# Pooled attention and a GELU MLP on one core: V fetched three groups ahead between two output stores, with another order of group 0

## The chip, the cores and the metric

The kernel runs on one core of one Trainium2 chip. The metric is the device time of one execution in microseconds (us); lower is better. TensorE (PE in the profile) multiplies matrices, VectorE (DVE), ScalarE (ACT) and GpSimd (POOL) do elementwise work, and SyncE (SP) issues nearly all transfers.

## The reference, cut to what matters

```python
# q, k, v: [8 batches, 8 heads, 576 positions, 64]; float32
k_p = k.reshape(B, H, 72, 8, 64).mean(axis=3)        # mean of each 8 positions
v_p = v.reshape(B, H, 72, 8, 64).mean(axis=3)
scores = q @ k_p.T / sqrt(64)                        # [576, 72] for each head
attn = softmax(scores)
x = (attn @ v_p), heads side by side                 # [4608, 512]
h = x @ w_in                                         # 512 -> 2048
g = gelu_tanh(h)
out = g @ w_out                                      # 2048 -> 512, [4608, 512]
```

## The kernel before, in words

The 4608 rows are worked through in nine groups of 512 rows. Groups 0 to 7 are the first 512 positions of each batch; a group called R gathers the last 64 positions of all eight batches. The order is 0, 1, 2, 3, 4, 5, 6, R, 7, and `n_` counts the place in that order.

The attention of the next group is hidden in the MLP of the current one. The MLP of a group is one long row of matmuls with numbered slots: slots 0 to 63 are the first layer (`hidden`, `hidden_two`, `hidden_fast`), slots 64 to 175 the second (`mlp`, L537 to L614; 7 products of 16 matmuls each). `at(hooks, slot, f, ...)` hangs a step in front of the matmul of that slot. This only sets the order in which instructions are written. Each engine then runs its own list in that order and waits where it needs another engine's result, and so does SP with its transfers. Nothing is rearranged later.

The steps that matter here, for the group after next or the next one:

- `load_kv` (L764) fetches the pooled operands' sources: K main part (1 MB), two halves of 128 KB, and V main part (1 MB), into a tile `kv` that has two buffers. `load_q` fetches 1 MB of queries. All are issued by SP, except the queries of R, which GpSimd issues.
- `pool` sums over 8 positions on VectorE in up to three adds (L149, L151, L152) and writes `kvb`. `k_transpose_dma` (L211) turns K's sums with a transposing transfer into `kTd`; `k_spread` (L218) lets GpSimd copy them into `kbd`. `spread_v` (L172) multiplies V's sums by masks into `vbd`.
- `cast_q` (L128) casts queries to bfloat16 in quarters; `q_transpose_dma` (L232) turns them into `qT`, `scores` (L248) multiplies, `exps` and `norm` (L257, L279) make the softmax in `eb`, `e_transpose_dma` (L306) turns it into `eT`, and `values` (L344) yields `xT`, the MLP's input.
- At the end of a group `store_pair` (L416) sends out two stores of 512 KB: the first after product 3 (of slots 144 to 159), the second after product 4 (slots 160 to 175), when ScalarE has copied its last part. Both read tiles named `osb`, of which there are two buffers.
- The fast groups (`hidden_fast`, places 3 to 8 of the order) use the same two `osb` buffers at their start as scratch: L501 writes one of them after the first product, L508 the other after the third. L508 can start when the second store of the group before has landed. It reads `x4`, an accumulator that TensorE continues at slot 28 (`S(3)`, a `c L475` group in the profile).

In `hidden_fast` the order of slots is: product into x4 (0 to 3), into y4 (4 to 7), two hidden blocks (8 to 15), `S(2)` into x4 (16), `S(1)` into y4 (20), a hidden block (24), `S(3)` into x4 (28), and so on.

Group 0 has nothing to hide behind: its attention is written out by hand (L640 to L749), in four blocks of 128 rows. Its copies out of PSUM go to VectorE or ScalarE as the argument says; `norm_two` splits a block's normalization between both; `spread_v` in three parts and the cast of blocks 2 and 3 go to GpSimd and VectorE. A one-element copy into `gate` (L720) makes GpSimd wait for block 0's normalization before it goes on with the second part of `spread_v`. Block 3's scores are hung into slot 4 of group 0's MLP (`first_s`), and `hidden_half` has an order of its own for its first eight matmuls, so that four of them need only the first half of `xT`.

Of the kernel before, what the change touches and what calls it, by code (L numbers as in the profile page):

```python
# [15 lines left out]
GELU_SET = "gelu_apprx_tanh_and_others"  # L16
# [3 lines left out]
def kernel(  # L20
# [21 lines left out]
    nc = tc.nc  # L42
# [4 lines left out]
    KO = DM // 128  # L47
# [3 lines left out]
    W = H * Sp  # L51
# [45 lines left out]
    def kv_tile(b):  # L97
        st[b]["kv"] = kvp.tile([128, NB, 8, D], F32, name="kv", tag="kv")
# [29 lines left out]
    def cast_q(g, j0, j1, eng):  # L128
        if "qb" not in st[g]:
            st[g]["qb"] = work.tile([128, 4, H, D], BF16, name="q_b", bufs=1)  # L130
        copy(eng, st[g]["qb"][:, j0:j1], st[g]["q"][:, :, j0:j1].rearrange("p h j d -> p j h d"))
# [91 lines left out]
    def q_transpose_pe(g, j, eng, tag):  # L223
        tp = psum.tile([128, HP, 128], BF16, name="tp", tag=tag, bufs=BUFS[tag])
        for pr in range(HP):
            nc.tensor.transpose(out=tp[:, pr, :],
                                in_=st[g]["qb"][:, j, 2 * pr:2 * pr + 2, :].rearrange("p h d -> p (h d)"),
                                identity=identb)
        copy(eng, st[g]["qT"][:, j], tp)
# [69 lines left out]
    def e_transpose_pe(g, j, eng, tag):  # L299
        tp = psum.tile([128, 5, 128], BF16, name="tp", tag=tag, bufs=BUFS[tag])  # L300
        for c in range(5):
            nc.tensor.transpose(out=tp[:, c, :], in_=eb[:, j, 128 * c:128 * c + 128], identity=identb)
        copy(eng, st[g]["eT"][:, j], tp)
# [83 lines left out]
    def hidden_half(g, fo, half, hook, s):  # L387

        c0 = 256 * half
        hp = psum.tile([128, 2, 256], F32, name="mm", tag="mm", bufs=4)  # L390
        order = [(0, 0), (0, 1), (1, 0), (1, 1), (0, 2), (0, 3), (1, 2), (1, 3)]
        for i, (f, ko) in enumerate(order if s == 0 else sorted(order)):
            hook(s + i)
            nc.tensor.matmul(out=hp[:, f, :], lhsT=w_in_b[:, ko, (fo + f) * 128:(fo + f + 1) * 128],  # L394
                             rhs=st[g]["xT"][:, ko, c0:c0 + 256],
                             start=(i == 0 if s == 0 else ko == 0), stop=(ko == KO - 1), skip_group_check=True)
        nc.scalar.activation(out=gT[:, fo:fo + 2, c0:c0 + 256], in_=hp, func=ACT.Gelu_apprx_tanh)

    def output(g, r, fo, o):
# [317 lines left out]
    norm_two(0, 0, 5)  # L717
    spread_v(0, nc.gpsimd, (0,))
    pool_pe(0, 7, 9, 1, nc.scalar)
    nc.gpsimd.tensor_copy(out=gate, in_=eb[:, 0, 128 * 5 - W:128 * 5 - W + 1])  # L720
    spread_v(0, nc.gpsimd, (1,))
    cast_q(0, 2, 3, nc.gpsimd)
    spread_v(0, nc.gpsimd, (2,))
    load_w_in(2)
    load_w_in(3)
    norm_two(0, 1, 5)
    e_transpose_pe(0, 0, nc.vector, "mm")
    q_transpose_pe(0, 2, nc.scalar, "mm")
    e_transpose_pe(0, 1, nc.vector, "mm")
    scores(0, 2)  # L730
    exps(0, 2)
    cast_q(0, 3, 4, nc.vector)
    for x in range(2):
        values_half(0, 0, x, [nc.vector, nc.scalar][x], "mm")
    q_transpose_pe(0, 3, nc.vector, "mm")

    def first_s():
        scores(0, 3)
        exps(0, 3)
        nc.scalar.preload_act_table_set(GELU_SET)  # L740
        norm(0, 2, nc.vector)
        norm(0, 3, nc.vector)

    def first_t(j):
        e_transpose_pe(0, j, nc.vector, "sc")
# [18 lines left out]
    def load_kv(n, parts=(0, 1)):  # L764
        if n != B - 1:
            b = B - 1 if n == R else n
            if 0 in parts:
                kv_tile(b)
                load_main(b, "k", 0, 4, nc.sync)
                load_half(b, "k", nc.sync)  # L770
                load_half(b, "v", nc.sync)
            if 1 in parts:
                load_main(b, "v", 0, 4, nc.sync)

    def at(hooks, s, f, *a):
        hooks.setdefault(s, []).append(lambda: f(*a))
# [4 lines left out]
        at(hooks, va, values, n, (0, 1), False)  # L781

    hooks = {}
    at(hooks, 4, first_s)
    at(hooks, 16, first_t, 2)
    at(hooks, 28, first_t, 3)
    at(hooks, 32, first_v)
# [43 lines left out]
    for n_, g in enumerate(seq):  # L831
        if n_ == 0:
            continue
        hooks = {}
        fast = n_ >= 3
        if n_ == 1:
            for i in range(1, 4):
                at(hooks, i, w_sums, i, 0, NP, nc.vector)
            at(hooks, 36, g_sums, 0, 4)
            at(hooks, 57, g_sums, 4, 6, (0,))  # L840
        elif fast:
            at(hooks, 41, g_sums, 0, 2, (0,))
            at(hooks, 57, g_sums, 2, 6, (0,))
            at(hooks, 65, g_sums, 6, 8, (0,))
            at(hooks, 65, g_sums, 0, 4, (1,))
        else:
            at(hooks, 20, g_sums, 0, 2)
            at(hooks, 36, g_sums, 2, 4)
            at(hooks, 57, g_sums, 4, 6, (0,))
        if not fast:  # L850
            at(hooks, 65, g_sums, 6, 8, (0,))
        at(hooks, 64 + 32, g_sums, 4, 8, (1,))
        if n_ + 1 < len(seq):
            n = seq[n_ + 1]
            b = B - 1 if n == R else n
            kv = n != B - 1
            if n_ == 1:
                for j in range(4):
                    at(hooks, 22 + 4 * j, cast_q, n, j, j + 1, nc.scalar)
                at(hooks, 35, qT_tile, n)  # L860
                at(hooks, 35, q_transpose_dma, n)
            if kv and not fast:
                t0 = 22 if n_ == 1 else 12
                at(hooks, t0, pool, b, 0, 5)
                at(hooks, t0, dup_k, b, 0, 5)
                at(hooks, t0, kT_tile, b, None)
                at(hooks, t0, k_transpose_dma, b)
                t1 = t0 + (16 if n_ == 1 else 24)
                at(hooks, t1, pool, b, 5, 9)
                at(hooks, t1, k_spread, b, [nc.gpsimd, nc.gpsimd])  # L870
                at(hooks, t1, spread_v, b, nc.gpsimd)
            elif kv:
                at(hooks, 5, pool, b, 0, 5, (0,))
                at(hooks, 17, pool, b, 0, 5, (1,))
                at(hooks, 17, dup_k, b, 0, 5)
                at(hooks, 17, kT_tile, b, None)
                at(hooks, 17, k_transpose_dma, b)
                at(hooks, 17, spread_gated, b)
                at(hooks, 40, k_spread, b, [nc.gpsimd, nc.gpsimd])
            if fast:  # L880
                at(hooks, 2, qT_tile, n)
                at(hooks, 2, q_transpose_dma, n)
            sc_at = [68, 68, 90, 90]
            for j in range(4):
                at(hooks, sc_at[j], scores, n, j)
                at(hooks, sc_at[j] + 1, exps, n, j)
            at(hooks, 80, eT_tile, n)
            for j in range(4):
                at(hooks, 80 if j < 2 else 92, norm, n, j, nc.vector if j > 1 else nc.gpsimd)
                at(hooks, 80 if j < 2 else 92, e_transpose_dma, n, j)  # L890
            at(hooks, 64 + 66, nc.scalar.preload_act_table_set, GELU_SET)
            at(hooks, 64 + 100, xT_tile, n)
            if n_ == 1:
                at(hooks, 64 + 100, values, n, (0,))
                at(hooks, 64 + 107, values, n, (1,))
            else:
                at(hooks, 64 + 104, values, n)
        if n_ + 2 < len(seq):
            n2 = seq[n_ + 2]
            s2 = 44 if n_ == 1 else 57  # L900
            for half, ahead in enumerate((3, 2)):
                if n_ + ahead < len(seq) and seq[n_ + ahead] == R:
                    if half == 0:
                        at(hooks, 9, q_tile, R)
                    at(hooks, 9, gate_queries, g)
                    at(hooks, 9, load_q, R, 2 * half, 2 * half + 2, nc.gpsimd)
            if n2 != R:
                at(hooks, s2, q_tile, n2)
                at(hooks, s2, load_q, n2, 0, 4, nc.sync)
            at(hooks, 64 + 52, cast_gated, n2)  # L910
            if n_ < 2:
                at(hooks, 64 + 100, qT_tile, n2)
                at(hooks, 64 + 100, q_transpose_dma, n2)
                at(hooks, 64 + 100, load_kv, n2, (1,))
            elif n2 != B - 1:
                b2 = B - 1 if n2 == R else n2
                at(hooks, 64 + 84, pool, b2, 5, 9, (0,))
                at(hooks, 64 + 97, pool, b2, 5, 9, (1,))
            if n_ == 1:
                at(hooks, 45, load_kv, n2, (0,))  # L920
            else:
                at(hooks, 28, load_kv, n2)
        mlp(g, hooks, n_ + 1 == len(seq), fast)


# [28 lines left out]
```

## Time and profile before

| What | Value |
|---|---|
| Time, median of 3 runs | 280.57 us (279.7 to 280.78) |
| The profiled execution's own time | 280.57 us |
| Its span in the profile | 278.6 us |
| Granted TensorE clock | 0.998 of full speed |
| PE busy | 269.8 us (97% of the span) |
| DVE busy | 221.7 us (80%) |
| ACT busy | 176.1 us (63%) |
| POOL busy | 81.9 us (29%) |
| Moved by transfers | 54.37 MB, 195 GB/s over the span |

How to read it: the difference of about 2 us between span and time lies around the profiled part. PE is busy for all but 8.8 us of the span. So a change pays only where it removes one of PE's few idle stretches, and it costs where it makes a new one. A transfer has two times in the profile: when SP issues it, and when it lands.

### The profile page before, as it was taken

Reading aid. Unit: us, or ns where it says so; the run is one execution under the profiler, and the core shown is the slowest. Engines: PE = TensorE matmul, PEld = TensorE weight load, DVE = VectorE, ACT = ScalarE, POOL = GpSimd, SP = SyncE. Lnnn points to the kernel's source line nnn. Section 1 sums busy time; section 2 is a strip of 40 time slices with the busy share of each in tenths; the row PEclk is TensorE's granted clock in tenths of the full one; section 3 lists DMA queues with packets and bytes.
Section 4 is the critical chain, followed back from the end, with each engine's and each line's share of the span. In section 5 each row is a group of like instructions: output and inputs, shape, how many; then the busy total and the mean of one; then the engine's idle time right before and its main releaser. Section 6 shows DMA issues by size and latency. Waiting matters only on the chain.

```text
span 278.6 us, 6579 instructions
## 1 busy us (share of the span) xinstructions
PE 269.8 (97%) x2686; PEld 192.2 (69%) x2686; DVE 221.7 (80%) x367; ACT 176.1 (63%) x264; POOL 81.9 (29%) x123
## 2 busy tenths in 40 slices
PE   7989999998999999999999999999999999999995
PEld 3678844445854588668866876588668966886684
DVE  5896869989956798989999979887989558955832
ACT  1576575588547764696469636955696469656820
POOL 4640282006510542314263445533223300300000
PEclk9999999999999999999999999999999999999999
DMA  7999999998999895999399978964752460243013
GB/s 227 310 189 287 367 385 226 301 353 212 233 223 243 258 279 137 175 303 249 120 218 271 279 138 209 238 194 122 166 161 49 125 151 2 49 101 99 1 41 113
DMA packets 67856, 54.37 MB, mean 195 GB/s; under 512 B 41458, under 2 KB 53746, under 8 KB 67826
## 3 DMA queue, kind: packets, MB, share of 16 engines
q1 hardware_dynamic: 65186, 50.67, 71.3%
q0 software_dynamic: 2496, 3.15, 6.1%
q8 instruction: 21, 0.34, 0.5%
q10 hardware_dynamic: 144, 0.13, 0.1%
q14 instruction: 9, 0.07, 0.1%
HBM read 36.70 MB, written 9.44 MB: 166 GB/s over the span
## 4 chain that ended last, share of the span: by engine, by line
PE 78%; DMA 9%; DVE 7%; ACT 2%; POOL 1%; SPq 1%; issue 1%; DVEq 0%; ACTq 0%
PE mm L587 29%; PE mm L383 17%; PE c L475 11%; PE mm L400 5%; PE mm L394 5%; PE xo L344 3%; PE x L587 3%; DMA kTd<-kvb 2%; DMA q_sb<-in_q_dram 2%; PE sc L248 2%; DMA qT<-q_b 2%; DMA out_dram<-osb 1%; DMA eT<-eb 1%; PE mm L532 1%; DVE den L264 1%; DVE eb L279 1%
## 5 line engine op out<-in xcount | busy, mean ns | idle before, releaser
L383 PE MATMUL mm<-xT,w_in_b 128*128 128x512 bf16 x304 | 70.0, 379 | 0.0
L587 PEld LDWEIGHTS <-gT 128*128 128x128 bf16 x512 | 48.3, 98 | 9.0 <-issue 1.4
L385 ACT ACTIVATE gT<-mm 128x512 bf16<-128x512 f32 x76 | 43.6, 599 | 14.6 <-PE mm L383 14.4
L383 PEld LDWEIGHTS <-w_in_b 128*128 128x128 bf16 x304 | 29.7, 98 | 30.9 <-issue 0.3
L587 PEld LDWEIGHTS <-stage 128*128 128x128 bf16 x384 | 37.6, 98 | 4.4
L92 ACT CAST xT<-xo 128x512 bf16<-128x512 f32 (+1 forms) x24 | 13.2, 610 | 29.1 <-PE xo L344 24.8
L587 PE MATMUL mm<-tw,gT 128*128 128x256 bf16 x240 | 30.0, 273 | 0.0
L587 PE MATMUL mm<-w_out_b,gT 128*128 128x256 bf16 x240 | 29.9, 273 | 0.0
L264 DVE TENSOR_REDUCE den<-e 128x8 f32<-128x576 f32 x36 | 26.3, 731 | 3.3 <-ACT e L257 3.3
L279 POOL TENSOR_TENSOR eb<-e,r 128x576 bf16<-128x576 f32 x14 | 15.8, 1150 | 44.5 <-DVE r L273 23.7
L257 ACT ACTIVATE e<-sc 128x576 f32<-128x576 f32 x36 | 22.4, 650 | 8.7 <-POOL eb L279 4.3
L92 ACT COPY osb<-mm 128x512 f32<-128x512 f32 x30 | 17.8, 592 | 15.1 <-PE mm L587 14.4
L587 PE MATMUL mm<-tw,stage 128*128 128x256 bf16 x224 | 26.7, 273 | 0.0
L149 DVE TENSOR_TENSOR kv<-kv 128x1024 f32<-128x1024 f32 (+3 forms) x19 | 22.6, 1190 | 4.1 <-DMA kv<-in_k_dram 2.6
L172 POOL TENSOR_TENSOR vbd<-kvb,vmask 128x256 bf16<-128x256 bf16 (+2 forms) x38 | 22.0, 600 | 5.6 <-DVE kvb L152 4.7
L475 PEld LDWEIGHTS <-ws 128*128 128x128 bf16 x192 | 18.8, 98 | 6.4 <-issue 0.6
L94 POOL CAST q_b<-q_sb 128x1024 bf16<-128x1024 f32 (+1 forms) x15 | 16.1, 1094 | 19.7 <-DMA q_sb<-in_q_dram 19.6
L94 POOL COPY kbd<-kTd 64x288 bf16<-64x288 bf16 x12 | 7.0, 585 | 36.8 <-DMA kTd<-kvb 36.5
L475 PE MATMUL c<-tt,ws 128*128 128x256 bf16 x144 | 17.7, 272 | 0.1
L435 DVE TENSOR_TENSOR stage<-gT 128x512 bf16<-128x512 bf16 (+1 forms) x25 | 13.7, 548 | 4.8 <-ACT gT L385 2.7
L279 DVE TENSOR_TENSOR eb<-e,r 128x576 bf16<-128x576 f32 x18 | 16.6, 920 | 0.6
L394 PE MATMUL mm<-xT,w_in_b 128*128 128x256 bf16 x128 | 15.6, 273 | 0.1
(107 smaller groups left out, 421.3 us busy)
## 6 DMA issues: line engine op xcount, KB each, us to landing
kv<-in_k_dram SPq DMA_DIRECT2D x7, 1024.0 KB, 7.8
q_sb<-in_q_dram SPq DMA_DIRECT2D x7, 1024.0 KB, 9.8
kv<-in_v_dram SPq DMA_DIRECT2D x6, 1024.0 KB, 9.5
out_dram<-osb SPq DMA_DIRECT2D x12, 512.0 KB, 3.1
out_dram<-osb SPq DMA_DIRECT2D x11, 256.0 KB, 3.3
kv<-in_v_dram SPq DMA_DIRECT2D x4, 512.0 KB, 10.2
w_in_b<-in_moe_w_in_dram POOLq DMA_DIRECT2D x4, 512.0 KB, 6.7
w_out_s<-in_moe_w_out_dram SPq DMA_DIRECT2D x2, 1024.0 KB, 13.6
```

Of the source, the lines that this page charges most:

```text
L92: eng.copy(out=out, in_=in_)
L94: eng.tensor_copy(out=out, in_=in_)
L149: add(out=t[:, :, 0:4, :], in0=t[:, :, 0:4, :], in1=t[:, :, 4:8, :], op=ALU.add)
L172: eng.tensor_tensor(out=vbd[p0:128, b, n0:n1, :].rearrange("p (c r) (hh d) -> p c (r hh) d", c=max(m, 1), d=D), in0=kvb[p0:128, 4 + c0:4 + ...
L257: nc.scalar.activation(out=e.rearrange("p (x h) s -> p x (h s)", x=2), in_=sc[:, :, 0:4 * Sp], func=ACT.Exp, scale=1.0 / 64.0)
L264: nc.vector.reduce_sum(out=den, in_=e, axis=AX.X)
L279: eng.tensor_tensor(out=o.rearrange("p (pr hh s) -> p hh pr s", hh=2, s=Sp), in0=e.rearrange("p (hh pr) s -> p hh pr s", hh=2), in1=r.rear ...
L383: nc.tensor.matmul(out=hp, lhsT=w_in_b[:, ko, fo * 128:(fo + 1) * 128], rhs=st[g]["xT"][:, ko, :], start=(i == 0), stop=(i == KO - 1))
L385: nc.scalar.activation(out=gT[:, fo, :], in_=hp, func=ACT.Gelu_apprx_tanh)
L394: nc.tensor.matmul(out=hp[:, f, :], lhsT=w_in_b[:, ko, (fo + f) * 128:(fo + f + 1) * 128], rhs=st[g]["xT"][:, ko, c0:c0 + 256], start=(i = ...
L475: nc.tensor.matmul(out=acc[:, m, :], lhsT=lhs(i, m), rhs=rhs(i), start=bool(fresh and i == 0 and m % 2 == 0), stop=(i == 1), skip_group_ch ...
L587: nc.tensor.matmul(out=xs[p] if acc is xs else acc[:, p, :], lhsT=lt, rhs=rt, start=bool(fresh and m == 0 and (p == 0 or (last and acc is ...
```

## The change

Three things are changed together.

First, V. Before, V's main part of the group two places ahead was fetched together with K, the halves and the queries, right after `kTd`'s transfer. After, from place 2 on, V of the group three places ahead is fetched at slot 175, which is between the two output stores on SP's list. This happens at the ends of places 2, 3 and 4 (groups 2, 3 and 4). At place 2 itself V of group 4 moves ahead of K of group 4 on SP's list.

Second, at place 1 the last quarter of group 2's queries is cast by GpSimd at slot 22, in place of ScalarE at slot 34; the other three stay on ScalarE at slots 22, 26 and 30.

Third, group 0: the wait on `gate` goes, GpSimd casts blocks 2 and 3 in one instruction of 128x1024, block 3's queries are turned before block 1's softmax, block 0's softmax is copied by ScalarE and block 2's queries by VectorE (they were the other way round), block 3's scores stand ahead of the MLP and not inside it, and the first hidden block has the plain order of matmuls.

```diff
@@ hidden_half
-        order = [(0, 0), (0, 1), (1, 0), (1, 1), (0, 2), (0, 3), (1, 2), (1, 3)]
-        for i, (f, ko) in enumerate(order if s == 0 else sorted(order)):
-            hook(s + i)
...
+        for f in range(2):
+            for ko in range(KO):
+                hook(s + 4 * f + ko)
...
@@ group 0
     spread_v(0, nc.gpsimd, (0,))
     pool_pe(0, 7, 9, 1, nc.scalar)
-    nc.gpsimd.tensor_copy(out=gate, in_=eb[:, 0, 128 * 5 - W:128 * 5 - W + 1])
     spread_v(0, nc.gpsimd, (1,))
-    cast_q(0, 2, 3, nc.gpsimd)
+    cast_q(0, 2, 4, nc.gpsimd)
     spread_v(0, nc.gpsimd, (2,))
...
-    e_transpose_pe(0, 0, nc.vector, "mm")
-    q_transpose_pe(0, 2, nc.scalar, "mm")
+    e_transpose_pe(0, 0, nc.scalar, "mm")
+    q_transpose_pe(0, 2, nc.vector, "mm")
+    q_transpose_pe(0, 3, nc.scalar, "mm")
     e_transpose_pe(0, 1, nc.vector, "mm")
     scores(0, 2)
     exps(0, 2)
-    cast_q(0, 3, 4, nc.vector)
     for x in range(2):
         values_half(0, 0, x, [nc.vector, nc.scalar][x], "mm")
-    q_transpose_pe(0, 3, nc.vector, "mm")
-
-    def first_s():
-        scores(0, 3)
-        exps(0, 3)
-        nc.scalar.preload_act_table_set(GELU_SET)
-        norm(0, 2, nc.vector)
-        norm(0, 3, nc.vector)
+    scores(0, 3)
+    sums(0, 2)
+    exps(0, 3)
+    nc.scalar.preload_act_table_set(GELU_SET)
+    norm(0, 2, nc.vector)
+    norm(0, 3, nc.vector)
...
-    at(hooks, 4, first_s)
@@ load_kv
+            if "kv" not in st[b]:
+                kv_tile(b)
             if 0 in parts:
-                kv_tile(b)
@@ place 1
-                    at(hooks, 22 + 4 * j, cast_q, n, j, j + 1, nc.scalar)
+                    at(hooks, 22 + 4 * (j % 3), cast_q, n, j, j + 1, nc.gpsimd if j == 3 else nc.scalar)
@@ loads of K and V
-            if n_ == 1:
-                at(hooks, 45, load_kv, n2, (0,))
-            else:
-                at(hooks, 28, load_kv, n2)
+            at(hooks, 45 if n_ == 1 else 28, load_kv, n2, (0,))
+            if n_ == 2:
+                at(hooks, 14, load_kv, n2, (1,))
+            if n_ > 1 and n_ + 3 < len(seq):
+                at(hooks, 64 + 111, load_kv, seq[n_ + 3], (1,))
```

More of the change, by code (lines that the diff above doesn't have):

```diff
@@ L390, in hidden_half @@
         hp = psum.tile([128, 2, 256], F32, name="mm", tag="mm", bufs=4)
-        order = [(0, 0), (0, 1), (1, 0), (1, 1), (0, 2), (0, 3), (1, 2), (1, 3)]
-        for i, (f, ko) in enumerate(order if s == 0 else sorted(order)):
-            hook(s + i)
-            nc.tensor.matmul(out=hp[:, f, :], lhsT=w_in_b[:, ko, (fo + f) * 128:(fo + f + 1) * 128],
-                             rhs=st[g]["xT"][:, ko, c0:c0 + 256],
-                             start=(i == 0 if s == 0 else ko == 0), stop=(ko == KO - 1), skip_group_check=True)
+        for f in range(2):
+            for ko in range(KO):
+                hook(s + 4 * f + ko)
+                nc.tensor.matmul(out=hp[:, f, :], lhsT=w_in_b[:, ko, (fo + f) * 128:(fo + f + 1) * 128],
+                                 rhs=st[g]["xT"][:, ko, c0:c0 + 256], start=(ko == 0), stop=(ko == KO - 1))
         nc.scalar.activation(out=gT[:, fo:fo + 2, c0:c0 + 256], in_=hp, func=ACT.Gelu_apprx_tanh)
```

## The prediction

> **What bounds the kernel now.** I read the busy line and the chain on the page first, then TensorE's timeline for its idle stretches, then who waits for transfers, then SP's list of issues.
>
> ```profile
> PE 269.8 (97%) x2686; PEld 192.2 (69%) x2686; DVE 221.7 (80%) x367; ACT 176.1 (63%) x264; POOL 81.9 (29%) x123
> PE 78%; DMA 9%; DVE 7%; ACT 2%; POOL 1%; SPq 1%; issue 1%; DVEq 0%; ACTq 0%
> ```
>
> PE is idle for 278.6 - 269.8 = 8.8 us in all. About 3.3 us of that lie after its last matmul (275.29). The timeline shows the idle stretches with their releasers in brackets; these five, and 1.07 and 0.69 us in the first 6 us, are the main ones:
>
> ```profile
> 14.48 0.40 PE L226 MATMUL tp<-identb,q_b 128*128 128x128 bf16 x4 [0.55 <-POOL q_b L94]
> 15.56 0.42 PE L241 MATMUL sc<-kbd,qT 128*128 128x144 bf16 x4 [0.23 <-ACT qT L92]
> 66.77 0.45 PE L248 MATMUL sc<-kbd,qT 64*64 64x72 bf16 x32 [0.83 <-DMA qT<-q_b]
> 163.90 0.97 PE L344 MATMUL xo<-eT,vbd 32*64 32x256 bf16 x24 [0.64 <-DMA eT<-eb]
> 180.15 0.45 PE L248 MATMUL sc<-kbd,qT 64*64 64x72 bf16 x30 [0.59 <-POOL kbd L94]
> ```
>
> After 17 us only 0.83 + 0.64 + 0.59 = 2.06 us of idle time can be won. So everything turns on new idle time. The chain shows where PE has no slack though it isn't idle:
>
> ```profile
> 110.68 4.04 DMA out_dram<-osb
> 114.82 1.02 ACT osb L508
> 115.84 0.04 issue
> 115.88 1.03 PE c L475 x8
> ```
>
> That is the start of place 3: the second store of place 2 lands at 114.72, L508 may then write `osb`, and S(3) starts as L508 ends. A store that lands later there moves PE by as much. The waits agree (us in total, times, longest):
>
> ```profile
> ACT osb L508 <- DMA out_dram<-osb: 2.4, 3, 1.0
> ```
>
> **Part 1, group 0.** Removed: the gate copy (0.19) with its wait (0.58), two casts of 128x512 (GpSimd 0.61, VectorE 0.42). Added: one GpSimd cast of 128x1024; rows of that shape have a mean of 1.15, the slowest near here 1.51. The second half of q landed at 13.27, so the cast runs from 13.3 to 14.4-14.8; block 2's quarter alone was ready at 14.42. Block 3's query turn (0.41 on PE) now stands ahead of block 1's softmax turn. On ScalarE the softmax copy (0.59 for 512 columns, so about 0.7 for 640, an estimate) and one query copy (0.59) queue behind the three normalizations that ended at 14.89: about 16.2, against 15.51 for the one copy before. Block 3's scores (0.25) move ahead of the first hidden matmul: equal work, so 17.28 + 0.25 = 17.53 is the mark to compare with. I get the first hidden matmul at 17.6 to 18.2, a loss of 0.1 to 0.7, taken 0.4. Without the gate VectorE's first normalization runs beside GpSimd: 0.83 as the second did, not 0.53; ScalarE's share ended at 13.42 anyway.
>
> This loss is covered by the 0.83 idle at 66.77. What releases PE there is a chain without PE: group 2's queries landed at 57.62, the casts start at 57.70. Their load was issued at 48.90, behind softmax turns that SP could not issue faster, because loads from the start (V of group 1) landed only at 46.10. If that cover were gone, the 0.4 would count in full.
>
> **Part 2, the cast at place 1.** The fourth ScalarE cast ran from 60.71 to 61.33 and `qT` was issued at 61.36. After, ScalarE's third ends near 60.33, and GpSimd, idle for the 17.4 us before 65.01, casts from 57.7 for 0.6 to 0.9 us (rows of 128x512: 0.61, 0.86). SP issues `kTd` from 59.62 to 60.84, so `qT` is issued at 60.9 at the earliest: 0.46 won at most. Against it: the trace's transfer records show `qT`'s packets from 64.0 to 66.1, following at once on `kTd`'s last (63.9), so the issue may not have been the limit. And VectorE's adds for `kTd` run beside the cast: an add of 128x1024 took 1.87 and 1.75 beside casts twice this long, 1.25 without, so half of 0.55 is 0.3 lost. I take 0.1 won (from 0.46 won to 0.2 lost).
>
> [...]
>
> **Part 3, V between the stores.** Bytes are unchanged. Each of three loads (ends of places 2, 3, 4) now stands ahead of the second store on SP's list. What a load in front of a store does is seen once in this trace, at the end of place 1:
>
> ```profile
> 82.43 0.57 SPq L112 DMA_DIRECT2D kv<-in_v_dram  x1
> 83.09 0.49 SPq L416 DMA_DIRECT2D out_dram<-osb  x1
> 84.41 1.77 SPq L211 DMA_TRANSPOSE kTd<-kvb  x1
> ```
>
> That store's landing, then the one at 138.35, from the answers for the store's line in those windows:
>
> ```profile
> DMA to landing us min/median/max: 9.4/9.4/9.4
> DMA to landing us min/median/max: 3.0/3.0/3.0
> ```
>
> In the packet records V's 512 packets of 2 KB run from 83.6 to 88.4 and the store's 4 KB packets begin as they end: the queue works in order. At a steady rate (95 packets in 0.5 us, from 120 on) V needs 2.7 us; this one, with a slow start, needed 4.8. At place 1 that hurt nobody, since place 2 isn't fast and writes `osb` late. The three new ones precede fast places.
>
> Place 3: the first store's packets end at 110.25. V then holds the queue until 112.95 to 115.05; the second store's began at 111.45. Delay 1.5 to 3.6, slack none: 2.4 taken, between the ends, as the loads after transposes start slowly but not all as slowly as that one.
>
> Place 4: first store's packets end at 137.95, V until 140.7 to 142.8, second store's began at 139.15: delay 1.55 to 3.65. Slack: landing 141.35 to L508 at 141.84 is 0.5, and L508's end to S(3) another 0.5. Cost 0.5 to 2.6, taken 1.4.
>
> Place 5: 165.05, then 167.75 to 169.85, against 167.55: delay 0.2 to 2.3; slack 0.9 likewise. At the same time the 0.64 idle at 163.90 goes: `eT` was issued at 159.88 and took 4.0 to land, against 2.6 in undisturbed places, because q landed only at 160.04; with V's 2.7 us out of that burst it lands before PE asks. But PE then comes 0.64 sooner to the same store, and the slack shrinks by it. Cost 0 to 2.0, less 0.64: taken +0.2 in sum (-0.64 to +1.4). Late next: `kTd`, whose landing at 178.26 made the 0.59 at 180.15. It queues behind `qT`, which queues behind that store: 0 to 1.0, taken 0.3.
>
> [...]
>
> Place 2's V of group 4 ahead of K: both were already issued back to back behind `kTd` (86.23 to 89.67) and neither is needed before place 3's first slots; K landed at 95.93, so V's 2.7 us are hidden. Taken at nothing; if K's pool at 111.09 waited it would cost PE only through `kTd`, 60 slots later.
>
> Sum: -0.1 + 2.4 + 1.4 + 0.2 + 0.3 = +4.2. The profiled execution took 280.57, which is also the median of the runs: 284.8 us. The ends: -0.46 + 1.5 + 0.5 - 0.64 = +0.9, and 0.2 + 3.6 + 2.6 + 1.4 + 1.0 = +8.8, so 281.5 to 289.4 in this case.
>
> **Rivals.** (a) The store isn't held: V drains before the second store's packets would start, or the engines overlap them. Then the 0.64 goes, and 0.1 to 0.46 at place 1: 279.5 to 279.8. With the 0.59 at 180.15 gone too, 278.9. For it: at place 5 the stores are 4 us apart, and the first store's packets leave the queue empty at 138.0 to 139.0. Against it: 9.4 us. It decides if V holds the queue under about 1.2 us, and no row shows that.
>
> (b) The store is held, but L508's delay is caught up: PE finds other idle time to give back. Against it: after place 5 PE has almost none. It would leave at most 1 us: 281 to 282.
>
> (c) Group 0's loss isn't covered and is the only effect beside (a): 280.0 to 280.6.
>
> **How the numbers follow.** The store held, as summed: 0.70. (b) 0.08, (a) 0.15, (c) 0.07. About 0.5% (1.4 us) is what a measurement of this kernel can tell from no change, so faster means below 279.17: half of (a), 0.08. Same is the rest of (a), (c), and some of (b) and of the low end of the main case: 0.20. Slower: 0.72. Range: 279.6 to 288.0 leaves out most of (a)'s faster half and the case of all upper ends together.
>
> **What would show it.** Right: the second stores of places 2, 3 and 4 land 5 to 7 us after issue; ACT osb L508 waits for out_dram by 2 to 4 us at places 3 and 4; PE idle before c L475 there, released by L508; the idle at 163.90 gone; PE's other work unchanged. Wrong: second stores landing in 3 to 4 us, L508 waiting under 1 us, or idle time before the first hidden matmul that carries through 66 us.

## The result, and the profile after

The changed kernel takes 289.02 us (median of 6, 287.41 to 290.63) against 280.13 us (279.02 to 281.25) for the kernel before: a ratio of 1.031, 95% interval 1.026 to 1.036. It is slower, as forecast, but by 8.9 us and not by 4.2; that is above the top of the range (288.0). The profiled execution took 288.41 us with a span of 286.7 us, 8.1 us more span than before.

From the page of the changed kernel, the busy line and the chain's shares:

```profile
PE 271.6 (95%) x2686; PEld 192.9 (67%) x2686; DVE 222.1 (77%) x365; ACT 175.3 (61%) x264; POOL 80.1 (28%) x123
PE 75%; DMA 16%; DVE 4%; ACT 3%; issue 1%; SPq 1%; POOL 0%; ACTq 0%; DVEq 0%
```

PE's idle time grew from 8.8 to 15.1 us (286.7 less 271.6), and transfers now hold 16% of the chain instead of 9%. PE is also busy 1.8 us longer with the same 2686 matmuls. These are two effects. The idle stretches come first, from TensorE's timeline (start, us, what ran; in brackets the idle time before it and its releaser):

```profile
67.02 0.45 PE L248 MATMUL sc<-kbd,qT 64*64 64x72 bf16 x32 [0.60 <-DMA qT<-q_b]
119.24 1.03 PE L474 MATMUL c<-tt,ws 128*128 128x256 bf16 x8 [3.17 <-ACT osb L507]
149.30 1.03 PE L474 MATMUL c<-tt,ws 128*128 128x256 bf16 x8 [2.44 <-ACT osb L507]
179.09 1.87 PE L474 MATMUL c<-tt,ws 128*128 128x256 bf16 x8 [2.09 <-ACT osb L507]
180.75 1.88 PE L383 MATMUL mm<-xT,w_in_b 128*128 128x512 bf16 x4
```

PE now stands before S(3) at places 3, 4 and 5: 3.17 + 2.44 + 2.09 = 7.70 us. The old stretches of 0.64 (before `xo`, 163.90) and 0.59 (180.15) are gone. L507 is the copy that was L508 before. The chain shows what it waits for, the second store of the group before:

```profile
110.92 7.16 DMA out_dram<-osb
...
141.71 6.43 DMA out_dram<-osb
...
171.85 6.08 DMA out_dram<-osb
...
179.09 1.87 PE c L474 x8
```

The stores land 7.16, 6.43 and 6.08 us after their issue; at the first of these places it was 4.04 before. The waits (us in total, times, longest) agree: 2.4 us with a longest of 1.0 became

```profile
ACT osb L507 <- DMA out_dram<-osb: 11.4, 4, 4.1
PE c L474 <- ACT osb L507: 7.7, 3, 3.2
```

The second effect stands in the last two lines of the timeline: after the third idle stretch the same matmuls take 1.87 and 1.88 us instead of 1.03. The windows by engine have the granted clock in them (us, then busy time of PE, PEld, DVE, ACT and POOL, PEclk, DMA share, GB/s):

```profile
175.65:179.06 3.41, 1.35 (x9) 0.69 (x7) 2.42 (x4) 1.03 (x2) 3.27 (x7) 1.00 1.23 311
179.06:182.47 3.41, 3.38 (x13) 1.79 (x13) 1.23 (x1) 1.42 (x2) 1.91 (x4) 0.50 1.02 143
182.47:185.88 3.41, 3.41 (x25) 2.35 (x24) 2.20 (x4) 3.01 (x4) 0.84 (x2) 1.00 1.11 317
```

For 3.41 us the clock is halved: PE's 3.38 us of work there would have taken half as long, so 1.7 us are lost. In the profiled execution of the kernel before the clock record, which starts 4.4 us into the span, shows the whole clock until PE's last matmul is done.

The span's 8.1 us put together: +0.25 by the first scores of group 2 (67.02 against 66.77), +3.11 to S(3) of place 3, +2.60 at place 4, +1.35 at place 5 (1.99 of delay less the 0.64 gone), then +1.7 from the halved clock and -0.59 from the idle time gone at 180.15, and -0.3 in all the rest.

### The profile page after: what moved, and what is told of

Read it like the earlier page. It is cut to its first block, busy times and chain, and to the rows that moved or that the text cites. A ratio compares the mean times of both kernels' runs of the same rounds, so it can differ in the third digit from the quotient of the medians.

```text
span 286.7 us, 6575 instructions
## 1 busy us (share of the span) xinstructions
PE 271.6 (95%) x2686; PEld 192.9 (67%) x2686; DVE 222.1 (77%) x365; ACT 175.3 (61%) x264; POOL 80.1 (28%) x123
## 4 chain that ended last, share of the span: by engine, by line
PE 75%; DMA 16%; DVE 4%; ACT 3%; issue 1%; SPq 1%; POOL 0%; ACTq 0%; DVEq 0%
PE mm L586 30%; PE mm L383 19%; PE c L474 10%; DMA out_dram<-osb 7%; PE mm L399 5%; DMA w_out_s<-in_moe_w_out_dram 5%; PE x L586 2%; PE xo L344 2%; PE sc L248 2%; DMA q_sb<-in_q_dram 2%; DMA qT<-q_b 2%; PE mm L531 1%; ACT xT L92 1%; PE mm L394 1%; ACT osb L507 1%
## 5 line engine op out<-in xcount | busy, mean ns | idle before, releaser
L383 PE MATMUL mm<-xT,w_in_b 128*128 128x512 bf16 x304 | 71.0, 382 | 0.0
L279 POOL TENSOR_TENSOR eb<-e,r 128x576 bf16<-128x576 f32 x14 | 15.8, 1149 | 50.3 <-DVE r L273 28.3
L149 DVE TENSOR_TENSOR kv<-kv 128x1024 f32<-128x1024 f32 (+3 forms) x19 | 23.4, 1231 | 4.1 <-DMA kv<-in_k_dram 2.6
L92 ACT COPY osb<-mm 128x512 f32<-128x512 f32 x30 | 17.8, 593 | 14.2 <-PE mm L586 13.5
L474 PE MATMUL c<-tt,ws 128*128 128x256 bf16 x144 | 18.5, 280 | 7.7 <-ACT osb L507 7.7
L435 DVE TENSOR_TENSOR gT<-gT 128x512 bf16<-128x512 bf16 (+1 forms) x25 | 13.0, 519 | 3.5 <-ACT gT L385 1.4
```

Of the source, the lines that this page charges most:

```text
L92: eng.copy(out=out, in_=in_)
L149: add(out=t[:, :, 0:4, :], in0=t[:, :, 0:4, :], in1=t[:, :, 4:8, :], op=ALU.add)
L279: eng.tensor_tensor(out=o.rearrange("p (pr hh s) -> p hh pr s", hh=2, s=Sp), in0=e.rearrange("p (hh pr) s -> p hh pr s", hh=2), in1=r.rear ...
L383: nc.tensor.matmul(out=hp, lhsT=w_in_b[:, ko, fo * 128:(fo + 1) * 128], rhs=st[g]["xT"][:, ko, :], start=(i == 0), stop=(i == KO - 1))
L474: nc.tensor.matmul(out=acc[:, m, :], lhsT=lhs(i, m), rhs=rhs(i), start=bool(fresh and i == 0 and m % 2 == 0), stop=(i == 1), skip_group_ch ...
```

## Experiments

The theories have letters in the texts on record. **Q**: V's bytes stand in SP's queue ahead of the second store, and whatever next writes that store's buffer stops PE. **K**: a long idle stretch halves PE's clock for a while, which costs beside the idle time. **X**: R's queries, issued by GpSimd, and the transposing transfers, issued by SP, slow each other when they move together. **Y** and **Z** are two reasons why V holds the queue so long: because SP is issuing the transposing transfer right behind it (Y), or by itself (Z).

### One part alone

`e1_v_alone` is the kernel before with the change's edits to `load_kv` and to its calls, nothing else:

```diff
+            if n_ > 1 and n_ + 3 < len(seq):
+                at(hooks, 64 + 111, load_kv, seq[n_ + 3], (1,))
...
```

> The kernel before with the V loads of the change alone (place 2 at slot 14, and between the two stores at the ends of places 2, 3 and 4). Theory Q (the second store waits on SP's queue behind V's 1 MB, and L508 waits for the store): all of the loss is here; second stores of places 2 to 4 land 6 to 7.5 us after issue, PE idle before S(3) by 3.2, 2.4 and 2.1 us (each within 0.7), time 287 to 290. Theory G (group 0 or the cast carries a good part of the loss into the later groups): under 285.

Measured: 288.37 us, ratio 1.028 (1.021 to 1.035). In the profiled execution PE waits 3.54, 2.36 and 1.58 us for L508 before S(3) at places 3 to 5. `e2_without_v` is the changed kernel with V loaded as before, so group 0 and the cast alone:

```diff
-            at(hooks, 45 if n_ == 1 else 28, load_kv, n2, (0,))
...
+            if n_ == 1:
+                at(hooks, 45, load_kv, n2, (0,))
+            else:
+                at(hooks, 28, load_kv, n2)
```

> The changed kernel with the V loads put back as before, so group 0 and the cast alone. Theory Q: 280.1 plus 0.2 to 0.5, so 280.2 to 281, no idle time before S(3). Theory G: 283 or more.

Measured: 279.67 us, ratio 0.998 (0.992 to 1.004). So nearly the whole loss is V's place on the queue; group 0 and the cast together can't be told from nothing.

### Other places for the two transfers

`e3_v_after_store` issues V right behind the second store instead of ahead of it:

```diff
-                at(hooks, 64 + 111, load_kv, seq[n_ + 3], (1,))
+                last_load.append(seq[n_ + 3])
         mlp(g, hooks, n_ + 1 == len(seq), fast)
+        for n in last_load:
+            load_kv(n, (1,))
+        last_load.clear()
```

> The changed kernel with the three V loads issued right after the second store, not before it. Theory Q: second stores land in 3 to 4 us again, PE's idle before S(3) under 0.3 us at each place; qT and kTd queue behind V, so up to 1.5 us idle before the scores at places 3 to 5; time 279.5 to 282.5. Theory T (the first microseconds of a fast group can't bear another 1 MB in whatever order): the loss comes back before the scores, 285 or more.

Measured: 293.55 us, ratio 1.049 (1.043 to 1.055): worse, against what I expected. The store was free again (it landed 3.1 us after its issue) and the idle time before S(3) was gone, but PE now waited before the scores:

```profile
156.11 0.27 PE L248 MATMUL sc<-kbd,qT 64*64 64x72 bf16 x2 [5.14 <-POOL kbd L94]
191.19 0.27 PE L248 MATMUL sc<-kbd,qT 64*64 64x72 bf16 x2 [4.87 <-POOL kbd L94]
```

V's bytes had moved ahead of `qT` and `kTd`, and at places 4 and 5, where GpSimd issues R's queries, those ran at the same time as `qT`. In the packet records R's 128 packets of 4 KB took 751 and 799 ns each on the mean at these two places, against 251 and 234 in the kernel before, where `qT` was already through, and 159 for those of a store alone. Of `qT`'s 256-byte packets 2 to 126 started in each 0.5 us there, instead of 400 to 570. `qT` landed 15.8 us after its issue (174.62 to 190.43). At place 3, which has no such queries, there was no wait.

`e4_store_on_act` takes the store away from V by another queue: ScalarE issues it.

```diff
-                store_pair(g, 1, osb[1])
+                store_pair(g, 1, osb[1], eng=nc.scalar if g in (2, 3, 4) else nc.sync)
```

> The changed kernel with the second store of groups 2, 3 and 4 issued by ScalarE instead of SP; V stays where it is. Theory Q (order on one queue): the store no longer stands behind V, shares the engines with it and lands 3.5 to 5.5 us after issue; idle before S(3) 0 to 1.5 us at each place, time 280.5 to 284. Theory B (the bytes themselves, not their order, fill the engines): the store still lands after 6 us or more, time 287 or more.

Measured: 300.14 us, ratio 1.072 (1.065 to 1.079), the worst of all and not the 280.5 to 284 that I expected. ScalarE's timeline at place 3:

```profile
111.05 0.37 ACTq L415 DMA_DIRECT2D out_dram<-osb  x1
111.76 1.02 ACT L500 COPY osb<-c 128x1024 f32<-128x1024 f32 x1 [0.74 <-DMA out_dram<-osb]
...
122.62 1.01 ACT L507 COPY osb<-c 128x1024 f32<-128x1024 f32 x1 [8.40 <-DMA out_dram<-osb]
```

The store landed 11.5 us after its issue. Its first packet began only at 115.00, 3.95 us after the issue, among V's last ones. Then its packets ran beside `qT`'s on SP's queue until 122.06: 20 of the 128 took 0.5 to 3.3 us each, the others 0.16 to 0.28. `qT` landed 14.2 us after its own issue. So here a second queue was no way past the first: the store took 11.5 us in place of the 7.16 of the changed kernel, and `qT` 14.2 in place of 9.2.

### Is it the buffer, and does it go by bytes?

`e5_scratch_swapped` lets the fast places meet the held buffer later, at slot 36 instead of S(3) at 28:

```diff
-        k2, k0, k1 = part(), part(), spare
+        k2, k0, k1 = part(), spare, part()
```

> The changed kernel with the scratch of a fast group swapped: L507 (the former L508) writes the spare buffer, and the tile of the second store is first written by the VectorE copy L510, which TensorE needs only at slot 36. V stays between the stores. Theory Q (the late store costs time only through that one wait): V and the stores land as in the changed kernel (second store 6 to 7.2 us after issue), but PE's idle time before slot 28 goes, and before slot 36 1.7 us less is left per place, so 1.5, 0.7 and 0.4 us; time 281 to 284. Theory D (transfers in general are late, and the next wait takes over in full): 287 or more.

Measured: 284.10 us, ratio 1.016 (1.010 to 1.022). The stores land nearly as late as in the changed kernel (6.65 us after issue at place 3, 6.0 at places 4 and 5), but PE waits at slot 36, and less:

```profile
118.44 1.03 PE L474 MATMUL c<-xT,ws 128*128 128x256 bf16 x8 [1.14 <-DVE osb L510]
146.99 1.03 PE L474 MATMUL c<-xT,ws 128*128 128x256 bf16 x8 [0.45 <-DVE osb L510]
175.73 1.03 PE L474 MATMUL c<-xT,ws 128*128 128x256 bf16 x8 [0.53 <-DVE osb L510]
```

The wait went where the buffer went. `e6_half_of_v` leaves half of V between the stores and fetches the other half behind K:

```diff
-                at(hooks, 64 + 111, load_kv, seq[n_ + 3], (1,))
+                at(hooks, 64 + 111, load_kv, seq[n_ + 3], (1,), (0, 2))
+            if 2 < n_ < 6:
+                at(hooks, 28, load_kv, n2, (1,), (2, 4))
```

> The changed kernel with half of V (512 KB) between the stores and the other half at slot 28 of the next place, behind K. Theory Q by bytes: the store lands some 2.5 us sooner than in the changed kernel, idle before S(3) 0.7, 0.2 and 0 us, time 280 to 282.5. Theory P (any load there costs a fixed part, not by bytes): idle before S(3) 2 us or more at each place, time 286 or more.

Measured: 280.68 us, ratio 1.004 (1.001 to 1.006). The store at place 3 lands 4.63 us after its issue, and PE waits for it at one place only:

```profile
PE c L474 <- ACT osb L507: 0.6, 1, 0.6
```

With half the bytes the 7.70 us are 0.63. Both runs carry Q.

### The clock

`e8_filler` keeps PE busy with eight matmuls that nobody uses, ahead of S(3) at the three places:

```diff
+        if g in (3, 4, 5):
+            warm_up(8, "mm")
         product(x4, 0, S(3), T(t3), 28)
```

> The changed kernel with 8 matmuls of 128x512 on zeros (1.7 us) ahead of S(3) at places 3, 4 and 5: extra work for TensorE, in the time in which it waits. Theory K (idle time of 2 to 3 us costs a second time, because TensorE's granted clock is then halved for a stretch of 3.4 us, 1.7 us each): granted clock 0.998 or more, idle time that is left before S(3) under 1.5 us, time 285.5 to 287.5, below the changed kernel's 289. Theory N (the halved clock has nothing to do with idle time): clock still 0.98 to 0.994, time 288 to 291.

Measured: 287.22 us, ratio 1.028 (1.023 to 1.032). The store is held as before (ScalarE still waits 11.0 us for it in all), but the granted clock is 0.998 to 1.000 in all four executions, where all six of the changed kernel had 0.982 to 0.994. The loss of the medians is 7.4 us instead of 8.9. The difference of 1.5 us is near the 1.7 worked out from the trace, but the two intervals overlap, so that the times alone don't show it; the clocks do.

### R's queries

`e7_v_after_r_on_sp` is `e3_v_after_store` with R's queries issued by SP behind the gate's transfer, so that nothing moves on GpSimd's queue there; `e10_r_on_sp` is the same edit in the kernel before.

```diff
-                    at(hooks, 9, load_q, R, 2 * half, 2 * half + 2, nc.gpsimd)
+                    at(hooks, 28, load_q, R, 2 * half, 2 * half + 2, nc.sync)
```

> The run with V behind the second store, and R's queries (two times 512 KB at places 4 and 5) issued by SP behind kTd instead of by GpSimd. Theory X (a transposing transfer on SP's queue and a load on GpSimd's queue slow each other when they run together; V only pushed qT into R's loads): the 5 us idle before the scores at places 4 and 5 falls under 1.5 us each, qT lands within 9 us of its issue, time 280 to 285. Theory T (1 MB more at the start of a group is too much): idle time there stays 4 us or more, time 291 or more.

> The kernel before with R's queries issued by SP at slot 28, behind the gate's transposing transfer, instead of by GpSimd at slot 9; nothing else changed. If a copy on GpSimd's queue and a transposing transfer on SP's queue slow each other also where V is not between the stores, the idle of 0.64 us at 163.90 of before goes and the time falls by 0.3-1.0 us (278.8-279.6). If before's places leave enough time for both, the time does not change by more than 0.3 us.

Measured: 283.09 us, ratio 1.012 (1.008 to 1.015), and 282.89 us, ratio 1.013 (1.009 to 1.016). In the first the waits of some 5 us before the scores are gone, as X says; with the clock behind them they were worth some 10 us. The move also issues R's queries later (148.18 for 141.90 at place 4), behind `qT` and `kTd`. So it shows that their meeting with `qT` costs, not that it takes a second queue to make it costly. In the second the move itself costs: K then lands later and so do the queries and `eT`. The profiled execution of `e10_r_on_sp` had the whole clock and took 280.93 us; the other five had 0.986 to 0.994 and took 282.64 to 284.88, so most of the 2.7 us is probably the halved clock again. From the first one's timeline; the second has 1.13 and 0.59 at the same two places:

```profile
165.75 0.41 PE L344 MATMUL xo<-eT,vbd 32*64 32x256 bf16 x8 [1.70 <-DMA eT<-eb]
166.75 0.98 PE L344 MATMUL xo<-eT,vbd 32*64 32x256 bf16 x24 [0.59 <-DMA eT<-eb]
```

So my expectation for `e10_r_on_sp` (no change, or a gain) was wrong: with V where it was before there is no collision worth a move.

### Why V holds the queue 5 us

In the packet records V's 2 KB packets of place 3 run from 110.5 to 115.6, at 25 to 87 in each 0.5 us instead of the steady 95 that the prediction worked with. `e9_qt_later` was to part Y from Z:

```diff
-                at(hooks, 2, qT_tile, n)
-                at(hooks, 2, q_transpose_dma, n)
+                at(hooks, 14, qT_tile, n)
+                at(hooks, 14, q_transpose_dma, n)
```

> The changed kernel with the queries' transposing transfer (qT) of a fast place issued at slot 14 instead of slot 2, so that nothing transposing is queued on SP while V's 1 MB and the second store behind it move. Theory Y (V's packets are slow because the transposing transfer is being issued right behind them): V lands 5.0-5.7 us after its issue instead of 6.9-7.5, the second store 4.5-5.5 us instead of 6.1-7.2, PE's idle before S(3) shrinks to about 1.0 / 0.5 / 0.3 us, the clock stays whole, and the time is 282-285 us. Theory Z (V is slow by itself when it starts ahead of a store): V still lands 6.4 us or more after its issue, the idles stay near 3.2 / 2.4 / 2.1 us and the time is 287 us or more.

Measured: 287.90 us, ratio 1.029 (1.026 to 1.033). It parts nothing, and SP's timeline says why:

```profile
107.94 0.42 SPq L112 DMA_DIRECT2D kv<-in_v_dram  x1
110.46 0.36 SPq L415 DMA_DIRECT2D out_dram<-osb  x1
110.92 5.93 SPq L232 DMA_TRANSPOSE qT<-q_b  x1
```

A slot orders SP's list but doesn't time it: SP issued `qT` right behind the store all the same. `e13_q_copied` puts a plain copy of the same bytes in its place, and `e14_q_copied_before` does so in the kernel before:

```diff
-                at(hooks, 2, q_transpose_dma, n)
+                at(hooks, 2, q_copy, n)
```

> The changed kernel with the queries' transposing transfer of the fast places (group 2's place on) replaced by a plain copy of the same 512 KB from the same tile into the same tile: the queries are left untransposed there, so that part of the computation is left out, and the same work is done on wrong values. Theory Y (V's packets are slow because SP is issuing the transposing transfer right behind them): V lands 5.0-5.7 us after its issue instead of 6.9-7.5, the second store 4.5-5.5 us instead of 6.1-7.2, PE's idle before S(3) is 1.0 us or less at every place, and the time is 281-284 us. Theory Z (V is slow by itself between the stores): V still lands 6.4 us or more after its issue, the store 5.8 us or more, the idles stay at 2-3 us, and the time is 287 us or more.

> The control: the kernel before with the same plain copy in place of the transposing transfer in its fast places (the queries are left untransposed there). Theory Y: the second store, which lands 3.7-4.0 us after its issue in the kernel before where the transposing transfer is issued behind it, lands in 2.5-3.0 us, like the first store. Theory Z: it still takes 3.5 us or more. Either way the time stays within 1 us of the kernel before.

Measured: 289.42 us, ratio 1.035 (1.030 to 1.040), and 279.10 us, ratio 0.999 (0.996 to 1.002). With no transposing transfer behind it V still lands 8.6, 6.6 and 6.1 us after its issue (7.5, 7.4 and 6.9 in the changed kernel). The stores behind it take 7.7, 5.7 and 5.2 us (7.2, 6.4 and 6.1). In the kernel before, without V, they land in 3.60, 2.65 and 2.67 us with the plain copy against 4.04, 3.00 and 3.05. So Y is worth some 0.4 us on a store, up to 0.9 with V ahead of it, and not at every place: at place 3 the store landed 0.5 us later with the plain copy. The main part is not Y. That leaves Z, but no run had nothing at all behind V. From the transfers of the changed kernel at place 3 (KB each, us from issue to landing):

```profile
kv<-in_v_dram SPq DMA_DIRECT2D x1, 1024.0 KB, 7.5
```

and of `e13_q_copied`:

```profile
kv<-in_v_dram SPq DMA_DIRECT2D x1, 1024.0 KB, 8.6
```

Why 1 MB that starts between two stores moves at about half its steady rate stays open; the records don't tell the DMA engines apart.

### V elsewhere, and the parts that help put together

`e15_v_before_first_store` issues V ahead of both stores, at place 3 at 106.25 instead of 108.55:

```diff
-                at(hooks, 64 + 111, load_kv, seq[n_ + 3], (1,))
+                at(hooks, 64 + 88, load_kv, seq[n_ + 3], (1,))
```

> The changed kernel with V's load issued ahead of the first store (slot 88 of the second half instead of slot 111), about 2.1 us earlier on SP's queue; everything else as it is. If the cost is V's total time on the queue (theory Q): V starts 2.1 us earlier, so the second store lands some 2 us earlier, 4.5-5.2 us after its issue; the idles before S(3) fall from 3.2 / 2.4 / 2.1 us to 1.0 / 0.4 / 0.1 us, the clock stays whole, and the time is 281-284 us. If it is the place between the stores that is slow, whatever stands there: V lands within 5.5 us of its issue. If V, ahead of the first store, collides with the exponentials' transposing transfers (eT) instead: eT lands later than 107.5 us, PE waits before xo (slot 104 of the second half), and the time is 285 us or more.

Measured: 286.06 us, ratio 1.023 (1.015 to 1.031). The second store landed sooner (5.31 us after its issue), as Q says, but now the first store was held too, and its buffer is the one that L500 writes at the start of a fast place:

```profile
115.04 1.03 PE L474 MATMUL c<-tt,ws 128*128 128x256 bf16 x8 [1.86 <-ACT osb L500]
145.30 1.03 PE L474 MATMUL c<-tt,ws 128*128 128x256 bf16 x8 [1.90 <-ACT osb L500]
175.37 1.03 PE L474 MATMUL c<-tt,ws 128*128 128x256 bf16 x8 [1.63 <-ACT osb L500]
```

None of my alternatives named that: it is Q at the other buffer.

`e11_half_and_swap` and `e12_full_v_swap` have group 0 of before and the cast on GpSimd, the swapped buffers and R's queries on SP; the first has half of V between the stores, the second the whole of it and the later slot for `qT`.

```diff
-        k2, k0, k1 = part(), part(), spare
+        k2, k0, k1 = part(), spare, part()
...
-                    at(hooks, 9, load_q, R, 2 * half, 2 * half + 2, nc.gpsimd)
+                    at(hooks, 28, load_q, R, 2 * half, 2 * half + 2, nc.sync)
...
+                at(hooks, 64 + 111, load_kv, seq[n_ + 3], (1,), (0, 2))
```

> Group 0 as before; the last quarter of group 2's queries cast by GpSimd; of V, 512 KB between the stores and the other half at slot 28 behind K; the scratch buffers in the other order (the held store's buffer is met at slot 36 instead of S(3)); R's queries issued by SP behind the gate's transfer. The second store is held 4.6 us or less, which the 2 x 1.03 us of slots up to 36 cover: no idle before S(3) or slot 36, eT's wait of 0.64 us gone, R's collision gone. Theory Q with X: 278.4-279.6 us, as fast as before or up to 0.5% faster. If a half V costs something beyond its hold on the queue: 280.3 us or more.

> Group 0 as before; the full V between the stores; the scratch buffers in the other order; qT issued at slot 14; R's queries issued by SP behind the gate's transfer; the cast on GpSimd. Theory Q with Y: the store lands within 5.5 us of its issue, the wait at slot 36 shrinks to nothing or 0.3 us a place, and the time is 278.5-280.5 us. Theory Q with Z: the waits at slot 36 stay at 0.4-1.5 us a place, and the time is 282-284 us.

Measured: 281.19 us, ratio 1.005 (1.002 to 1.007), and 282.76 us, ratio 1.010 (1.006 to 1.013). In the first no store stops PE; what is left over before is `eT`'s wait, 0.94 and 0.61 us, which R's move made (as in `e10_r_on_sp`); the 278.4 to 279.6 us that I expected had counted that wait as gone. In the second PE waits 1.61 and 0.76 us at slot 36, as Q with Z says. None of the versions beats the kernel before.

## Why the prediction was right in its sign and wrong in its size

**The mechanism** was right: the second store held behind V, L507 late, PE idle before S(3) at places 3 to 5, the 0.64 gone, nothing else of PE's work changed. `e1_v_alone`, `e5_scratch_swapped` and `e6_half_of_v` show it.

**The step that failed is V's hold on the queue**, the term of Part 3 with ends of 2.7 and 4.8 us. I took the middle for each place "as the loads after transposes start slowly but not all as slowly as that one". From first to last packet V held the queue 5.1, 5.0 and 4.7 us at places 3, 4 and 5 (110.54 to 115.65, 141.48 to 146.50, 171.53 to 176.23). The only row that showed a load ahead of a store, place 1, was the one to go by, and I read even that too short: V's last packet ended there at 89.33 and not at 88.4, after the store's first had begun at 88.15. Nor did the queue pass from V to the store at once. At place 3 the store's first packet came 2.5 us later than before (114.02 for 111.53), about as taken; but V's last packets still ran among the store's, whose own last one ended 3.6 us later (117.47 for 113.88), and L508 waits for that one. At place 5 the text also counted on a gap between the stores in which V could move unnoticed: they were issued 3.94 us apart before, and 2.60 us after. So place 3 cost 3.11 and not 2.4, place 4 2.60 and not 1.4, place 5 1.35 net and not 0.2: 7.06 in place of 4.0. With the upper ends of the text the three would have summed to 7.6, the case that the range left out. The rate of 95 packets in 0.5 us that made the lower end is that of a stream already running; K's loads of the same size, in the trace of before, took 6.2 us and more from issue to landing, which should have warned me.

**The halved clock was in no term**: +1.7 us in the profiled execution, without which its 288.41 us would have been 286.7, below the top of the range, and up to three such stretches by the granted clocks of the six executions (one stretch of 3.41 us lowers the mean over 286.7 us by 0.006: 0.994 is one, 0.982 three). The clocks of `e8_filler`, 0.998 to 1.000 where these were 0.982 to 0.994, show that the idle time makes them.

**`kTd`** was taken at +0.3 and turned out at -0.59: PE came so late to place 5's scores that `kTd` had time.

**Group 0** was right: the first hidden matmul began at 17.83, in the 17.6 to 18.2 given and 0.3 after the mark of 17.53. That the 0.83 idle at 66.77 covers it was half wrong: PE arrived there 0.48 later (66.42 for 65.94), the idle time fell by 0.23 only, and 0.25 came through, since VectorE's adds for `kTd` move with the MLP too and were longer (one took 1.15 for 0.83).

**The cast** was taken at 0.1 won and won nothing. The lost half of VectorE's add was right, though: 0.83 became 1.15 beside the cast of 0.61.

```profile
58.21 1.15 DVE L151 TENSOR_TENSOR kv<-kv 128x640 f32<-128x640 f32 x1
```

The add began at 58.21, and the cast ended at 58.69: of the 0.48 us beside it the add lost 0.32. `kTd` was issued 0.66 us later than before and `qT` behind it 0.30 later, so the earlier cast met the limit that the text named, SP's list.

**Rivals.** (a), the store not held, fell with the 3.17 us of idle time before S(3) at place 3. (b), the delay caught up, gave 0.3 us over the rest of the span and 0.59 at 180.15, not 7. (c), group 0 as the only effect, is `e2_without_v`: nothing measurable.

## What to carry to other kernels

A load put ahead of a store on the same queue can cost whoever next writes the store's buffer the load's time on the queue, less the time in which the queue would have been empty and the slack of that writer: here 3.1, 2.6 and 1.4 us of some 5 us each. Size it by the packets of a like load in the same place of a trace, first to last, not by a steady packet rate. Half the bytes took away nearly all of the cost here (0.9 us left of 8.9), a later writer about half (4.3 us left). And an idle stretch of over 2 us on a busy TensorE should be priced with a halved clock that may follow: in the profiled execution the one of 2.09 us cost 1.7 us more, those of 3.17 and 2.44 us nothing more.

## What the runs showed of the hardware that was not expected

**In these profiles the clock was halved in stretches on a grid of 3.413 us, and it fell from whole to half only behind a window of that grid with 2.06 us or more of idle time.** In every run's clock record the halved stretches begin and end on one grid of 3.413 us, counted from the record's first change; in the changed kernel's the clock is whole for 174.08 us, halved for 3.413 and whole for 105.81, which is 51, 1 and 31 times 3.413. With that grid laid over PE's timeline in all 17 profiles, from 20 us on and up to PE's last matmul, this comes out. At whole clock, the 11 windows with 2.06 us or more of idle time (from 2.06 in the changed kernel to 3.41 in `e4_store_on_act`) were all followed by a halved one; the 20 windows with 0.93 to 1.96 us were all followed by whole clock. In a halved stretch less kept it halved: 1.60 us did in `e4_store_on_act` and 1.08 in `e1_v_alone`, while after 0.47 in `e9_qt_later` the clock was whole again. So in these runs one stretch of idle time cost or didn't by how it fell on the grid. In the changed kernel the idle time of 3.17 us at 116.07 fell half into each of two windows, and the clock stayed whole:

```profile
114.20:117.62 3.42, 1.87 (x14) 1.14 (x12) 2.94 (x5) 0.00 (x0) 1.25 (x4) 1.00 1.26 239
117.62:121.03 3.41, 1.79 (x13) 1.21 (x13) 0.66 (x1) 2.46 (x3) 1.44 (x3) 1.00 1.14 199
121.03:124.44 3.41, 3.41 (x25) 2.29 (x24) 2.82 (x5) 3.06 (x4) 0.84 (x2) 1.00 0.95 324
```

The shorter one of 2.09 us fell almost wholly into one window and halved the next, as shown above.

**A transfer on a second queue beside a transposing one on SP's queue was slow for both**: R's 4 KB packets took 0.75 and 0.80 us on the mean in `e3_v_after_store` instead of 0.25 and 0.23, a store of 512 KB landed in 11.5 us in `e4_store_on_act` instead of 3 to 4, of which nearly 4 went by behind V, and `qT` landed in 15.8 and 14.2 us in these two runs instead of 5 to 6. Whether the transposing makes it or any two queues would do so was not tried.
